# All scores of the first sequence in float32, from q and k laid out along partitions by the host

## The chip, the cores and the metric

The program runs on one core of a Trainium2 chip. A core has five engines that run their own instruction streams in order: TensorE (PE, matmuls; its weight loads are listed as PEld), VectorE (DVE), ScalarE (ACT), GpSimd (POOL) and SyncE (SP), which here issues nearly all DMAs. Engines wait for one another through semaphores. The metric is the device time of one execution in microseconds; the time of the kernel before is 735.77 us, the median of 3 runs (735.07 to 739.84).

## What is computed

Block-causal attention over 4 sequences with 8 heads, 576 rows and a head size of 64, then a dense layer of two matmuls with an ELU between them, then a top-1 mixture of 8 experts with a skip decision per row. Only the attention is touched here:

```python
B, H, S, D = q.shape                     # 4, 8, 576, 64
scores = scale * np.matmul(q, k.transpose(0, 1, 3, 2))     # scale 1/8
mask = block_i >= block_j                # blocks of 64 rows
scores = np.where(mask, scores, -1000000000.0)
scores = scores - np.max(scores, axis=-1, keepdims=True)
attn = np.exp(scores)
attn = attn / (np.sum(attn, axis=-1, keepdims=True) + 1e-09)
return np.matmul(attn, v).astype(np.float32)
```

Rows of the attention's result are put one sequence after the other into a matrix of 2304 x 512, which goes through the dense layer (512 to 2048 to 512) in 9 chunks of 256 rows.

## The kernel before

All instructions up to the experts are recorded first and then issued in an order that a planner chooses (`Recorder.order`): it knows what each step reads and writes, has an estimated duration for each kind of step, and gives each engine the step that can start first, with ties by the place in the program. Nearly every instruction thus carries the line of the recording helper, L320; rows are told apart by the names of tiles. A change of any step's cost, queue or buffer can move the order everywhere behind it.

**Attention.** A unit of `s_unit` (line 741) is one head of one 128-row tile n of queries (n = 0 to 3), or, for the last 64 rows (n = 4), a pair of heads, one in each half of the output's partitions. A pair p has two heads, and four pairs make the 8 heads. `x_unit` takes the maximum of a unit's scores (DVE, `mx`) and the exponential (ACT, `e`), `h_unit` and `l_unit` divide by the sum and split the result into two float16 halves (`ehl`, ACT and DVE), a transposing DMA turns them (`et`), and `pv` multiplies with the values (PE, `xps`), whose result is copied to `xt`, the input of the dense layer. Groups of units: g = 0 is n = 0 and 1 (rows 0 to 255, chunk 0 of the dense layer), g = 1 is n = 2 and 3 (chunk 1), and for sequence 0 g = 2 is n = 4.

**Scores by float16 halves.** For most tiles a row tile of q or k is loaded as it lies in memory (`raw`, 5 buffers), split into two float16 halves on ACT and DVE (`prep_k` writes `k1`, `prep_q` writes `qq`), and turned by a DMA transpose (`kt`, `qt`). The halves of 64 elements stand above each other in 128 partitions. For q a second copy with the halves swapped is made by two more DMAs (`qt<-qt`). Two matmuls per unit then give all four products of halves. The transposes and the swaps stand in SP's queue, in the planned order, with the loads of the dense layer's weights (`rw`), which come in an 8-byte format and are turned to float32 by three DVE instructions for each half (`twi`, `two`).

**Scores in float32.** For sequence 0 and n = 0 and 1 (`early`) the host hands over q and k of the first 256 rows once more, as `q0` and `k0` of 128 x 1024 with the two heads of a pair along the partitions. `load_early` (line 687) loads them without transposes. The q of one head is a tile whose other 64 partitions are zero, so that one float32 matmul with the k of both heads gives that head's scores. k of these rows is loaded and split to float16 as well (`prep_k`, b = 0, n = 0 and 1), since the tiles n = 2 to 4 need it.

**Dense layer.** For chunks 0 and 1 both matmuls run in float32 (`h<-xt,twi`, `y<-two,g`), from chunk 2 on in float16 halves of scaled weights. Chunk 1 can start when all four pairs of g = 1 have been multiplied with the values. Small matmuls `bm` and `cn` serve maxima and column norms for the scales, `lp` the routing. Sums of squares of weights (`sq`, `junk`) and of v (`vflat`) run on ACT.

## Time and profile before

| | |
|---|---|
| median of 3 runs | 735.77 us |
| the profiled execution | 739.56 us, its span 737.8 us |
| PE busy | 677.5 us (92%) |
| DVE busy | 575.0 us (78%) |
| ACT busy | 509.4 us (69%) |
| POOL busy | 79.3 us (11%) |
| moved by DMA | 133.99 MB |

Times in rows are microseconds from the span's start. PEclk is TensorE's granted clock as a share of full speed: 0.5 is the lower of two levels, and a value between is a mix over the stretch. A float32 matmul has two entries in the trace, so counts of float32 matmuls are twice those in the code. What stands in brackets behind a row is the time the engine stood idle before it and what ended that.

### The profile page before, as it was taken

Reading aid. Unit: us, or ns where it says so; the run is one execution under the profiler, and the core shown is the slowest. Engines: PE = TensorE matmul, PEld = TensorE weight load, DVE = VectorE, ACT = ScalarE, POOL = GpSimd, SP = SyncE. Lnnn points to the kernel's source line nnn. Section 1 sums busy time; section 2 is a strip of 40 time slices with the busy share of each in tenths; the row PEclk is TensorE's granted clock in tenths of the full one; section 3 lists DMA queues with packets and bytes.
Section 4 is the critical chain, followed back from the end, with each engine's and each line's share of the span. In section 5 each row is a group of like instructions: output and inputs, shape, how many; then the busy total and the mean of one; then the engine's idle time right before and its main releaser. Section 6 shows DMA issues by size and latency. Waiting matters only on the chain.

```text
span 737.8 us, 17507 instructions
## 1 busy us (share of the span) xinstructions
PE 677.5 (92%) x6553; PEld 466.8 (63%) x6553; DVE 575.0 (78%) x1646; ACT 509.4 (69%) x1086; POOL 79.3 (11%) x118
## 2 busy tenths in 40 slices
PE   6798984999989898989999999999999999999894
PEld 4585442776467656647657667667576677677683
DVE  5979898788989897888969965999778654675553
ACT  5755479899886886777758744767366556786682
POOL 1000000010000100100100010000106033323112
PEclk9799995799999999999999999999999999999998
DMA  9799999866798969979429447917065878998631
GB/s 299 247 259 282 387 270 234 179 142 138 155 176 144 185 154 211 169 142 202 91 42 176 98 59 206 376 58 226 32 201 145 222 162 195 218 275 150 224 117 16
DMA packets 213739, 133.99 MB, mean 182 GB/s; under 512 B 178171, under 2 KB 179205, under 8 KB 213120
## 3 DMA queue, kind: packets, MB, share of 16 engines
q1 hardware_dynamic: 208592, 123.85, 68.3%
q0 software_dynamic: 3952, 6.70, 4.5%
q10 hardware_dynamic: 1088, 2.10, 0.8%
q8 instruction: 56, 0.92, 0.5%
q14 instruction: 51, 0.42, 0.2%
HBM read 74.12 MB, written 12.75 MB: 118 GB/s over the span
## 4 chain that ended last, share of the span: by engine, by line
DMA 28%; PE 25%; issue 24%; DVE 14%; ACT 3%; SPq 2%; POOL 2%; POOLq 0%; DVEq 0%; ACTq 0%
PE h L320 10%; DMA out_dram<-o,gp 9%; PE y L320 8%; DMA gpa<-pay_d,ah 7%; DMA et<-ehl 4%; PE s L320 3%; DMA lst_d<-li,si 3%; PE xps L320 3%; DVE ehl L320 3%; DVE mx L320 2%; SPq L320 2%; DVE two L320 2%; DMA qt<-qt 2%; DVE twi L320 1%; DVE el L320 1%
## 5 line engine op out<-in xcount | busy, mean ns | idle before, releaser
L320 PE MATMUL h<-xt,win 128*128 128x256 f16 x1344 | 158.0, 273 | 1.0 <-DVE n L320 1.0
L320 PE MATMUL y<-wout,g 128*128 128x512 f16 x672 | 155.7, 379 | 0.0
L320 PEld LDWEIGHTS <-win 128*128 128x128 f16 x1344 | 129.0, 98 | 22.5 <-DVE n L320 1.1
L320 PEld LDWEIGHTS <-g 128*128 128x128 f16 x672 | 64.0, 98 | 66.6
L320 ACT ACTIVATE e<-s,mx 128x512 f32<-128x512 f32 (+4 forms) x160 | 82.0, 515 | 16.7 <-DVE ehl L320 6.9
L320 DVE TENSOR_REDUCE mx<-s 128x1 f32<-128x512 f32 (+4 forms) x160 | 74.7, 476 | 21.7 <-PE s L320 20.5
L320 ACT ACTIVATE ehl<-e,su 128x512 f16<-128x512 f32 (+4 forms) x144 | 74.0, 560 | 15.0 <-DVE su L320 9.0
L320 DVE SCALAR_TENSOR_TENSOR ehl<-e,su,ehl 128x512 f16<-128x512 f32 (+4 forms) x144 | 75.4, 552 | 3.3 <-ACT ehl L320 3.0
L320 PE MATMUL s<-kt,qt 128*128 128x384 f16 (+5 forms) x352 | 63.1, 314 | 11.8 <-ACT e L320 9.9
L320 PE MATMUL h<-xt,twi 128*128 128x256 f32 x256 | 64.6, 409 | 2.9 <-DVE g L320 2.7
L320 PE MATMUL y<-two,g 128*128 128x512 f32 x128 | 58.5, 599 | 0.6 <-DVE two L320 0.6
L320 PEld LDWEIGHTS h<-xt,twi 128*128 128x128 f32 x256 | 51.4, 206 | 11.8 <-DVE g L320 3.1
L320 ACT ACTIVATE el<-h,col 128x512 f32<-128x512 f32 x56 | 38.2, 683 | 25.5 <-PE h L320 24.1
L320 PEld LDWEIGHTS <-vt 128*64 128x64 f16 x1368 | 38.1, 115 | 24.2 <-issue 15.8
L320 PE MATMUL xps<-et,vt 128*64 128x128 f16 (+1 forms) x1368 | 46.6, 219 | 7.4 <-DMA et<-ehl 3.9
L320 PEld LDWEIGHTS <-p 128*128 128x128 f16 x984 | 46.6, 98 | 10.6 <-issue 4.7
L320 ACT ACTIVATE g<-el,col 128x512 f16<-128x512 f32 x56 | 40.2, 718 | 17.2 <-DVE el L320 16.7
L320 PEld LDWEIGHTS <-qt 128*128 128x128 f16 (+1 forms) x352 | 26.1, 105 | 32.2 <-issue 18.4
L320 DVE SCALAR_TENSOR_TENSOR g<-el,col,g 128x512 f16<-128x512 f32 x56 | 41.7, 745 | 2.5 <-ACT g L320 2.4
L320 DVE SCALAR_TENSOR_TENSOR el<-h,col,el 128x512 f32<-128x512 f32 x56 | 41.8, 746 | 1.2
L1531 DVE SCALAR_TENSOR_TENSOR p<-p,n,p 128x1024 f16<-128x1024 f32 x32 | 40.6, 1281 | 2.5 <-ACT p L1530 2.4
L320 DVE TENSOR_TENSOR hh<-r,hh 128x256 f16<-128x256 f32 x36 | 15.0, 424 | 33.5 <-ACT hh L1676 32.7
(236 smaller groups left out, 1152.6 us busy)
## 6 DMA issues: line engine op xcount, KB each, us to landing
p<-in_moe_w_dram SPq DMA_DIRECT2D x45, 512.0 KB
rw<-in_moe_w_in_dram SPq DMA_DIRECT2D x16, 512.0 KB
rw<-in_moe_w_out_dram SPq DMA_DIRECT2D x16, 512.0 KB
pb<-in_moe_w_dram SPq DMA_DIRECT2D x10, 512.0 KB
vflat<-in_v_dram SPq DMA_DIRECT2D x4, 1152.0 KB
out_dram<-pay SPq DMA_DIRECT2D x18, 256.0 KB
pay_d<-pay SPq DMA_DIRECT2D x18, 256.0 KB
raw<-in_k_dram SPq DMA_DIRECT2D x16, 256.0 KB
```

Of the source, the lines that this page charges most:

```text
L320: rec.call(e, time, lambda: getattr(self.real, op)(*args, **kw), reads, writes, dma)
L1531: rc.call("dve", 1.2, lambda: nc.vector.scalar_tensor_tensor(out=half(1), in0=raw.t, scalar=sc, in1=half(0), op0=ALU.mult, op1=ALU.subtrac ...
```

## The change

The short path of the first 256 rows is extended to all 576 rows of sequence 0. `q0` and `k0` are now 128 x 2304. `load_q0(n)` and `load_k0(n)` bring one row tile each; all of k is one float32 tile in the place that the float16 `kt` of sequence 0 had, and a q tile holds both heads, each with the other head's partitions zero (by DVE for n = 0 and 1, by POOL after that). `prep_k` for sequence 0 is only the scaling by 1/8 on ACT, `prep_q` nothing. In `s_unit` a unit of n < 4 is one float32 matmul and the one for the mask; a pair of n = 4 is one float32 matmul for each head and each of its two parts. The first v tile moves to the other ring of buffers (`ehl`).

```diff
--- before.py
+++ after.py
@@ -662,6 +662,9 @@
         return 128 if n < 4 else 64
 
     def load_raw(nm, b, n):
+        if b == 0 and nm != "v":
+            (load_q0 if nm == "q" else load_k0)(n)
+            return
         src = {"q": q, "k": k, "v": v}[nm]
         r = trows(n)
         t = ap.tile([128, H, D], F32, tag="raw", bufs=5, name="raw")
@@ -684,25 +687,36 @@
 
     X0 = {}
 
-    def load_early():
-
-        X0["q"] = [ap.tile([128, 2, 4, 128], F32, tag="qt", bufs=3, name="qx") for h in range(2)]
-        X0["k"] = ap.tile([128, 2, 4, 128], F32, tag="ehl", bufs=2, name="kx")
+    def load_q0(n):
+
+        r = trows(n)
+        x = QT[0, n] = ap.tile([128, 2, 4, r], F32, tag="qt" if n < 4 else "qh", bufs=3 if n < 4 else 1, name="qx")
         for h in range(2):
-            nc.vector.memset(X0["q"][h][64 - 64 * h:128 - 64 * h], 0.0)
+            (rc.gpsimd if n > 1 else nc.vector).memset(x[64 - 64 * h:128 - 64 * h, h], 0.0)
+        for h in range(2):
+            rows = slice(64 * h, 64 * h + 64)
+            rc.sync.dma_start(out=x[rows, h].rearrange("p a t -> p (a t)"), in_=q0[rows, 512 * n:512 * n + 4 * r])
+
+    def k0_of(n):
+        return KT[0][:, 512 * n:512 * n + 4 * trows(n)]
+
+    def load_k0(n):
+
+        if n == 0:
+            KT[0] = ap.tile([128, 4 * S], F32, tag="kt0", bufs=1, name="kx")
+        rc.sync.dma_start(out=k0_of(n), in_=k0[:, 512 * n:512 * n + 4 * trows(n)])
+
+    def load_v0():
+
+        x = X0["v"] = ap.tile([128, 2, H, D], F32, tag="ehl", bufs=2, name="vx")
         for n in range(2):
-            rows = slice(64 * n, 64 * n + 64)
-            rc.sync.dma_start(out=X0["q"][n][rows].rearrange("p n a t -> p (n a t)"), in_=q0[rows, :])
-            rc.sync.dma_start(out=X0["k"][:, n].rearrange("p a t -> p (a t)"), in_=k0[:, 512 * n:512 * n + 512])
-        X0["v"] = ap.tile([128, 2, H, D], F32, tag="qt", bufs=3, name="vx")
-        for n in range(2):
-            rc.sync.dma_start(out=X0["v"][:, n].rearrange("p h d -> p (h d)"), in_=v[0, 128 * n:128 * n + 128].rearrange("p h d -> p (h d)"))
-            RAW["v", 0, n] = X0["v"][:, n]
-
-    def scale_early(n):
-        rc.scalar.activation(out=X0["k"][:, n], in_=X0["k"][:, n], func=AF.Copy, scale=0.125)
+            rc.sync.dma_start(out=x[:, n].rearrange("p h d -> p (h d)"), in_=v[0, 128 * n:128 * n + 128].rearrange("p h d -> p (h d)"))
+            RAW["v", 0, n] = x[:, n]
 
     def prep_k(b, n):
+        if b == 0:
+            rc.scalar.activation(out=k0_of(n), in_=k0_of(n), func=AF.Copy, scale=0.125)
+            return
         r = trows(n)
         raw = RAW.pop(("k", b, n))
         if n == 0:
@@ -713,6 +727,8 @@
         rc.sync.dma_start_transpose(out=KT[b][:, :, n * 128:n * 128 + r], in_=k1[0:r].rearrange("p h a d -> p (h a d)"))
 
     def prep_q(b, n):
+        if b == 0:
+            return
         r = trows(n)
         raw = RAW.pop(("q", b, n))
 
@@ -744,16 +760,21 @@
         n = i // 2
         w = 128 * (n + 1) if n < 4 else S
         parts = [(0, w)] if w <= 512 else [(0, 512), (512, w)]
-        if not early(b, n):
-            qt, kt = QT[b, n], KT[b]
+        qt, kt = QT[b, n], KT[b]
         mx = sm.tile([128, 4], F32, tag="mx", bufs=4, name="mx")
         tl = []
         for m, (a, e_) in enumerate(parts):
             t = ps.tile([128, e_ - a], F32, tag="s", bufs=3, name="s")
             rc.atom()
-            if early(b, n):
-                rc.tensor.matmul(out=t, lhsT=X0["q"][i % 2][:, n, p, :], rhs=X0["k"][:, 0:n + 1, p, :], start=True, stop=False)
-                rc.tensor.matmul(out=t[:, w - 64:w], lhsT=later16[:, 0:128], rhs=later16[:, 128:192], start=False, stop=True)
+            if b == 0:
+                rhs = (kt[:, 0:512 * min(n + 1, 4)].rearrange("p (n a t) -> p n a t", a=4, t=128)[:, :, p, :] if m == 0
+                       else kt[:, 2048 + 64 * p:2112 + 64 * p])
+                if n < 4:
+                    rc.tensor.matmul(out=t, lhsT=qt[:, i % 2, p, :], rhs=rhs, start=True, stop=False)
+                    rc.tensor.matmul(out=t[:, w - 64:w], lhsT=later16[:, 0:128], rhs=later16[:, 128:192], start=False, stop=True)
+                else:
+                    for h in range(2):
+                        rc.tensor.matmul(out=t[64 * h:64 * h + 64, :], lhsT=qt[:, h, p, :], rhs=rhs, start=True, stop=True)
                 tl.append(t)
                 continue
             for ps_ in range(2):
@@ -1341,17 +1362,19 @@
 
     VF = [4, 5, 6, 6, 7, 8, 9]
     rc.base = -300
-    load_early()
+    load_q0(0)
+    load_k0(0)
+    load_q0(1)
+    load_k0(1)
+    load_v0()
     setup_consts()
     for x0, x1, y in ((0, 64, -2048.0), (64, 128, 0.0), (128, 192, 4096.0)):
         rc.gpsimd.memset(later16[:, x0:x1], y)
-    scale_early(0)
-    scale_early(1)
+    prep_k(0, 0)
+    prep_k(0, 1)
     rc.base = 0
     load_to(8)
     vflat(0)
-    addex(0, L("k", 0, 0), L("k", 0, 1))
-    addex(3, P(prep_k, 0, 0), P(prep_k, 0, 1))
     ex[6][0:0] = [lambda: vmax(0), lambda: vscale(0)]
     addex(9, P(prep_v, 0, 0), P(prep_v, 0, 1))
     for x in range(6):
@@ -1979,7 +2002,8 @@
     for name in _INS + ['q0', 'k0']:
         a = inputs[name[0] if name in ('q0', 'k0') else name]
         if name in ('q0', 'k0'):
-            a = a[0, :, 0:256].reshape(4, 2, 2, 128, 64).transpose(1, 4, 2, 0, 3).reshape(128, 1024)
+            a = a[0].reshape(4, 2, 9, 64, 64).transpose(1, 4, 0, 2, 3).reshape(128, 4, 576)
+            a = _np.concatenate([a[:, :, 128 * n:128 * n + 128].reshape(128, -1) for n in range(5)], 1)
         elif name in 'qkv':
             a = a.transpose(0, 2, 1, 3)
         a = _np.ascontiguousarray(a)
```

Three places of the order that the planner now makes, as the built programs have it (buffer numbers are kept in some names). First SP's queue behind the first weights: `rw` are weights, `raw` tiles of q, k or v as they lie in memory, `kx` and `qx` those in float32. Before:

```order
L320 DMA vflat<-in_v_dram 128x2304
L320 DMA raw<-in_k_dram 128x512 x3
L320 DMA raw<-in_q_dram 128x512
L320 DMA rw<-in_moe_w_in_dram 128x2x512
L320 DMA raw<-in_v_dram 128x512
L320 DMA rw<-in_moe_w_in_dram 128x2x512
L320 DMA_TRANSPOSE kt<-k_172 128x8x128
L320 DMA_TRANSPOSE qt<-qq 128x8x128
L320 DMA raw<-in_k_dram 64x512
L320 DMA rw<-in_moe_w_in_dram 128x2x512 x2
L320 DMA raw<-in_k_dram 128x512
L320 DMA_TRANSPOSE kt<-k_173 128x8x128
```

The same queue, after:

```order
L320 DMA vflat<-in_v_dram 128x2304
L320 DMA kx<-in_k_dram 128x512
L320 DMA qx<-in_q_dram 64x512 x2
L320 DMA rw<-in_moe_w_in_dram 128x2x512
L320 DMA raw<-in_v_dram 128x512
L320 DMA kx<-in_k_dram 128x256
L320 DMA rw<-in_moe_w_in_dram 128x2x512
L320 DMA qx<-in_q_dram 64x256 x2
L320 DMA raw<-in_v_dram 64x512
L320 DMA rw<-in_moe_w_in_dram 128x2x512 x2
L320 DMA kx<-in_k_dram 128x512
L320 DMA raw<-in_v_dram 128x512
```

All q and k of sequence 0 are in the queue with the first weights, and the transposes of k and q that stood between weight loads are gone. Second, PE around the start of chunk 0 (`h<-xt,twi`), before:

```order
L320 MATMUL tp<-ident,en 128x128 x4
L320 MATMUL xps<-et,vx 64x128 x4
L320 MATMUL h<-xt,twi_174 128x256 x8
L320 MATMUL h<-xt,twi_207 128x256 x8
L320 MATMUL h<-xt,twi_238 128x256 x8
```

and after:

```order
L320 MATMUL tp<-ident,en 128x128 x4
L320 LDWEIGHTS ones_75
L320 MATMUL bm_189<-bmt,ones_75 128x1
L320 MATMUL xps<-et,vx 64x128 x4
L320 MATMUL s<-kx,qx 128x384
L320 LDWEIGHTS late
L320 MATMUL s<-late 128x64
L320 MATMUL h<-xt,twi_170 128x256 x8
L320 MATMUL h<-xt,twi_198 128x256 x4
L320 MATMUL s<-kx,qx 128x512
L320 LDWEIGHTS late
L320 MATMUL s<-late 128x64
```

A score unit of n = 2 (384 columns; two more stand a little ahead of these rows) is now in front of chunk 0, and units of n = 3 (512 columns) follow in the second of its eight steps, where before the first unit of n = 2 stood in the sixth and the first of n = 3 behind three of eight steps of y. Third, PE between the last y of chunk 0 and the 42 value products ahead of chunk 1. Before, the products follow these rows:

```order
L320 MATMUL lp<-wgs,x2t 128x9
L320 LDWEIGHTS ones_75
L320 MATMUL cn<-cb,ones_75 128x8
L320 LDWEIGHTS qt
L320 MATMUL s<-kt,qt 128x128
L320 LDWEIGHTS late
L320 MATMUL s<-late 128x64
L320 LDWEIGHTS qt
L320 MATMUL s<-kt,qt 128x128
```

and after, these:

```order
L320 MATMUL y<-two_362,g 128x512 x2
L320 MATMUL bm_322<-ident,col 1x128
L320 MATMUL s<-kx,qx 64x512 x2
L320 MATMUL bm_325<-ident,col 1x128
L320 MATMUL s<-kx,qx 64x64 x2
L320 LDWEIGHTS ones_75
L320 MATMUL bm_324<-bmt,ones_75 128x1
L320 LDWEIGHTS ones_75
L320 MATMUL cn<-cb,ones_75 128x8
L320 MATMUL s<-kx,qx 64x512 x2
L320 LDWEIGHTS ones_75
L320 MATMUL bm_327<-bmt,ones_75 128x1
```

Before, routing (`lp`) and the first scores of sequence 1 came ahead of these products, and all four pairs of n = 4; now the last y of chunk 0 is twelve rows ahead of them, with three and a half of the four pairs of n = 4 in front.

## Rows read from the trace of the kernel before

**Rows 1.** By stretches: stretch, length, busy time and count by engine, granted clock, DMA

```profile
core 0: us, PE busy (x) PEld busy (x) DVE busy (x) ACT busy (x) POOL busy (x), PEclk, DMA share, GB/s
0.00:32.00 32.00, 20.84 (x122) 13.43 (x122) 23.82 (x78) 20.72 (x62) 3.95 (x38) 0.91 0.84 292
32.00:60.00 28.00, 27.81 (x123) 23.20 (x121) 23.42 (x45) 14.46 (x28) 0.00 (x0) 0.93 0.92 241
60.00:80.00 20.00, 16.79 (x61) 9.30 (x60) 17.65 (x35) 8.28 (x16) 0.00 (x0) 0.91 1.02 310
80.00:106.00 26.00, 23.96 (x117) 11.20 (x119) 24.88 (x54) 19.00 (x36) 0.00 (x0) 1.00 1.09 335
106.00:134.70 28.70, 15.79 (x217) 10.56 (x217) 22.36 (x98) 25.50 (x62) 0.61 (x3) 0.59 1.09 233
134.70:140.00 5.30, 5.30 (x20) 4.32 (x16) 3.99 (x17) 4.26 (x10) 0.20 (x1) 0.63 1.04 212
140.00:200.00 60.00, 60.00 (x448) 39.57 (x447) 52.51 (x141) 55.95 (x130) 3.42 (x4) 1.00 0.68 143
```

**Rows 2.** PE's timeline: start, duration, what, count [idle time before, its end]

```profile
32.02 21.29 PE L320 MATMUL h<-xt,twi 128*128 128x256 f32 x88
...
62.75 5.41 PE L320 MATMUL h<-xt,twi 128*128 128x256 f32 x16 [2.74 <-DVE g L320]
...
80.67 0.59 PE L320 MATMUL s<-kt,qt 128*128 128x512 f16 x2 [1.15 <-DMA qt<-qt]
...
102.28 3.70 PE L320 MATMUL y<-two,g 128*128 128x512 f32 x8 [0.20 <-DVE two L320]
...
129.55 2.45 PE L320 MATMUL xps<-et,vt 128*64 128x128 f16 x42
...
134.69 5.62 PE L320 MATMUL h<-xt,twi 128*128 128x256 f32 x16
```

**Rows 3.** PE's timeline: score units in float32 and in float16

```profile
15.88 0.49 PE L320 MATMUL s<-kx,qx 128*128 128x128 f32 x2
...
16.23 0.69 PE L320 MATMUL s<-kx,qx 128*128 128x256 f32 x2
...
21.01 0.69 PE L320 MATMUL s<-kx,qx 128*128 128x256 f32 x2
...
21.57 0.68 PE L320 MATMUL s<-kx,qx 128*128 128x256 f32 x2
...
53.15 0.33 PE L320 MATMUL s<-kt,qt 128*128 128x384 f16 x1
...
53.86 2.75 PE L320 MATMUL h<-xt,twi 128*128 128x256 f32 x12
```

**Rows 4.** PE's timeline: float32 value products in half arrays; scores of n = 4

```profile
13.87 0.44 PE L320 MATMUL xps<-et,vx 128*64 128x128 f32 x4
...
16.88 0.66 PE L320 MATMUL xps<-et,vx 128*64 128x128 f32 x8
...
110.54 0.62 PE L320 MATMUL s<-kt,qt 128*64 128x512 f16 x4
...
111.20 0.30 PE L320 MATMUL s<-kt,qt 128*64 128x64 f16 x4
```

**Rows 5.** Groups of instructions from 0 to 140: busy time, mean ns of one

```profile
L320 ACT ACTIVATE sq<-twi 128x1024 bf16<-128x1024 f32 x8 | 8.4, 1045 | 0.1
...
L320 DVE SCALAR_TENSOR_TENSOR k<-raw,k 128x512 f16<-128x512 f32 x7 | 4.8, 684 | 0.0
...
L320 ACT ACTIVATE k<-raw 128x512 f16<-128x512 f32 x7 | 4.3, 620 | 0.2 <-DMA kt<-k 0.2
```

**Rows 6.** Chain of waits in order of time: start, duration, what

```profile
70.61 9.93 DMA qt<-qt
...
121.98 4.42 DMA et<-ehl
```

**Rows 7.** SP's timeline: issue of the first k tile

```profile
1.46 0.57 SPq L320 DMA_DIRECT2D kx<-in_k_dram  x1
```

## The prediction

> **What bounds the kernel now.** I read the kernel by stretches first, then the order of matmuls on TensorE (PE) inside them, then the chain of waits. From 140 us on PE is the bound: in the next 60 us it is busy all the time at full clock [rows 1], so what happens ahead of that is worth what it delays PE. Ahead of it PE loses time in two ways that add up: it stands idle, and its clock falls. I count both as lost time: a stretch minus its busy time times its granted clock. From [rows 1] this gives 13.0 us for 0 to 32 (32 - 20.84 x 0.91), 2.1 for 32 to 60, 4.7 for 60 to 80, 2.0 for 80 to 106, 19.4 for 106 to 134.7 and 2.0 for 134.7 to 140: 43.2 us in all. The rows of PE show what the stretches are [rows 2]. At 32.02 chunk 0 of the first expert layer starts (h, then y) and ends at 106; chunk 1 starts at 134.69, right behind the 42 value products (xps) of the last head pair of rows 256 to 511. So the 19.4 us are a wait of chunk 1 for attention. Inside chunk 0 two stalls stand out: 2.74 us on a VectorE (DVE) result and 1.15 us on the swapped q of row tile 3 [rows 2].
>
> Why is attention late? The chain of waits has a piece of 9.93 us that ends when the swap DMAs of that q land, and later a transposing DMA of 4.42 us [rows 6]. The scores of tile 3 could thus start only at 80, and everything behind them (maximum, exponential, split, transpose, value product) was pressed into 80 to 131. Meanwhile DVE was busy 88.3 of the 102.7 us of 32 to 134.7 (the sum of four stretches of [rows 1]), ScalarE (ACT) 25.5 of the last 28.7, and the DMA queues had a share of 0.84 to 1.09 from the start.
>
> **What the change costs PE.** Float32 scores take one product instead of two, but it is slower by column. A float32 unit of 128 columns takes 0.35 us (15.88 to 16.23), one of 256 0.56 (21.01 to 21.57): 0.21 per 128 columns [rows 3]. So 384 columns cost 0.77 and 512 cost 0.98. Two float16 units of 384 columns fill 53.15 to 53.86, 0.355 each [rows 3]; scaled by columns one of 512 is 0.47. With eight units of each width: 8 x (0.77 - 0.355) + 8 x (0.98 - 0.47) = 7.4 us more. Row tile 4 has four units of 576 columns in which two heads use half of the array each. The float32 value products have that form: four entries take 0.44 us, eight 0.66 [rows 4], so one 128-column product on both halves costs 0.22, and a unit 4.5 x 0.22 + 0.2 = 1.2. If the halves did not overlap it were 2.0. The float16 unit took 0.62 + 0.30 = 0.92 in a stretch with a granted clock of 0.59 [rows 1, 4]; at the higher of the two levels I estimate 0.65. That is 4 x 0.55 = 2.2 more, between 1.1 and 5.4. Sum: **9.6 us** (8.5 to 13) of added PE work.
>
> **What it removes elsewhere.** For sequence 0 five k tiles and three q tiles need no split: eight DVE instructions of 0.684 us (5.5 us) and eight on ACT of 0.620 (5.0 us, less three scalings of k that are new, 1.6 by their columns) [rows 5]. Eight transposing DMAs and six swaps leave SP's queue; of the loads, the pieces of q and k come as float32 in their final layout. SP ran in order, and the order of before shows weight loads (rw) and raw tiles standing behind the first k and q transposes; these are now plain loads with nothing ahead of them that waits for a computed half. Here the Trainium skill (Advanced Engine Details and Errata, section X-Bar Transpose) says that transposing DMAs are as fast as plain ones, 350 to 400 GB/s. By that rule the eight transposes are 1.8 MB and 5 us of queue time. The trace isolates no transpose in an empty queue: its 4.42 us for 393 KB [rows 6] is longer than the 1.1 that the rule gives, in a queue with other loads in it.
>
> **What moves, stretch by stretch.**
> *0 to 32.* q now comes in two loads per tile where there was one, so the first k is issued third instead of second, and the second k sixth instead of fourth. One issue takes about 0.6 us [rows 7] and PE's first scores wait for these tiles, so I add 1 us (0 to 1.2). On ACT, ahead of the last copy of chunk 0's input, the new order puts three sums of squares of 1.05 us [rows 5], two scalings of k (1.0 together, by the row of the k split and their columns) and two exponentials (1.2, likewise), and takes away two splits (1.2): 4.1 us net. ACT is busy 20.72 of 32 us [rows 1], so part of it falls into its gaps. With the first 1 us I estimate that h starts 3 us later. Three float32 scores of 0.77 fill 2.3 of these, which leaves 0.7. The stretch loses 13.0 + 1.7 = 14.7 (13 to 18).
> *Chunk 0.* The waits on q and, with DVE relieved just where its k and q splits stood around 61 us, most of the 2.74 us go: 8.8 becomes 5; I add 1 for score units that now sit between h and y and wait for their score buffers. 6 (3 to 10).
> *The gap before chunk 1.* Scores of tile 3 start beside h, not at 80, so three of the four pairs are through their value products before y ends. What is left is the last pair: its split, a transpose of about 4.4 us, 42 products. In the new order these 42 stand behind four small matmuls of the maxima (bm, cn), which wait for DVE and ACT results of the pay tile and of tile 4: about eight ACT instructions, an estimated 6 us by the widths and [rows 5], in parallel with the transpose. I take 5 us for gap and clock together, against 21.4 before; bounds 3 (the chain is early) and 21 (nothing is gained).
> *After it.* Routing, the first scores of sequence 1 and the vector work of two units of tile 4 are now behind the start of chunk 1: by the order an estimated 2 us of PE, 7 of DVE and 5 of ACT work. In 140 to 200 DVE is busy 52.5 of 60 us and ACT 55.95 [rows 1], so DVE's share just fits and ACT's not quite: 1.5 us (0 to 4).
>
> **The sum.** Lost time 14.7 + 6 + 5 + 1.5 = 27.2 against 43.2: 16.0 us won. Minus 9.6 of added PE work: 6.4 us less. The profiled execution took 739.56 us (span 737.8 and 1.8 around it), 3.8 above the median of 735.77. The same difference on the median gives 735.77 - 6.4 = **729 us**. About 1% (7.4 us) is what a measurement of this kernel can tell from no change, so the forecast lies at the edge of that.
>
> **The rivals.**
> *More is gained.* If nothing stalls chunk 0 and the last pair is early, the lost time is 14 + 4 + 3 = 21, the gain 22.2 - 9.6 = 12.6, the time 723. For it: DVE's queue loses 5.5 us where it was busy nine tenths. Against it: ACT's new early work.
> *The gap is ACT's, not q's.* In 106 to 134.7 ACT was busy 25.5 of 28.7 us, and the change takes only 3.4 us from it in all. If ACT's queue paces the last pair, the gap shrinks only to about 11.5; 33.7 lost, 9.5 won, 9.6 paid: 736, no change. Against it: from 32 to 80 ACT was busy only 22.7 of 48 us [rows 1], and scores that come earlier let its work move there. The rule of the Trainium skill on transposes speaks for this rival too, since by it the removed DMAs were cheap.
> *Slower.* The added PE work stands in front of the chain it should help: the last pair's scores lie on PE behind y and behind 5 to 6 us of longer scores, and its chain of maximum, exponential, split and transpose begins only then. If the gap stays as it was (the total lost time is 43 again), the 9.6 us are paid in full: 745. The point that decides is where chunk 1's first h stands. Before, it is at 134.69 with 2.0 us of slow clock behind it; afterwards the 2 us of moved PE work and the 1.5 above still follow. So it is break-even at about 133; the forecast puts it at 127; at 140.6 or later the kernel is slower by 1%.
>
> **How the numbers follow.** Forecast (725 to 734) 0.45; more gained 0.22; no change 0.20; slower 0.13. Faster by over 1% (below 728.4) takes all of the second and a good third of the first: 0.39. Slower by over 1% (above 743.1) takes most of the last: 0.11. Within 1%: 0.50. The range 721 to 741 leaves out the far end of the second and most of the last, under 0.2.
>
> **What would show it.** Right: chunk 0's h starts at about 35 behind three float32 scores; units of 384 and 512 columns at 0.77 and 0.98; no wait for a q DMA in chunk 0; y ends at 114 to 120; h of chunk 1 at 124 to 130 with a granted clock near 1 around it. Wrong: h starting after 38 (ACT's early work), a y stage with PE waiting for DVE or for score buffers, the 42 products held by the small matmuls beyond 132, units of tile 4 of 2 us, or idle time of PE between 130 and 200, where it had none from 134.7 on.

## The result, and the profile after

The changed kernel takes **714.99 us** (median, 714.26 to 716.24) where the kernel before took 735.42 (734.25 to 739.84): a ratio of 0.971 with a 95% interval of 0.968 to 0.975, 20.4 us less. Timed again beside the later experiments it was 0.975 (0.970 to 0.980). The forecast was 729 with a range of 721 to 741: the sign was right, the size was off by a factor of three. The profiled execution took 23.3 us less (a span of 714.5 for 737.8); that of before was one of its slower ones, which is where the 3 us between 23.3 and 20.4 lie.

The first rows are those of the changed kernel by stretches, cut where chunk 0 begins (38.1), where its last y ends (112.5), where chunk 1's first h stands (118.4), where the float16 chunks begin (194.4) and where their last h ends (547.6). They answer to [rows 1].

```profile
core 0: us, PE busy (x) PEld busy (x) DVE busy (x) ACT busy (x) POOL busy (x), PEclk, DMA share, GB/s
0.00:38.10 38.10, 26.44 (x132) 16.64 (x132) 27.19 (x86) 25.24 (x73) 6.59 (x44) 0.87 0.95 303
38.10:112.50 74.40, 74.40 (x376) 45.77 (x374) 68.01 (x148) 48.80 (x96) 0.00 (x0) 1.00 0.98 273
112.50:118.40 5.90, 4.46 (x62) 2.27 (x61) 5.00 (x31) 3.69 (x9) 0.41 (x2) 1.00 1.03 239
118.40:194.40 76.00, 75.25 (x587) 48.24 (x587) 69.24 (x212) 71.86 (x174) 5.25 (x6) 1.00 0.76 157
194.40:547.60 353.20, 347.10 (x3403) 236.86 (x3402) 304.37 (x921) 246.43 (x535) 26.31 (x36) 1.00 0.67 159
547.60:714.50 166.90, 151.02 (x2004) 115.02 (x2002) 94.78 (x247) 108.45 (x197) 43.37 (x37) 0.96 0.70 176
```

The same cut of the kernel before, for the part behind 134.7 that the prediction did not look at closely:

```profile
134.70:209.50 74.80, 73.99 (x522) 47.76 (x519) 65.62 (x176) 68.16 (x158) 3.83 (x6) 0.97 0.71 149
209.50:569.40 359.90, 347.15 (x3403) 237.38 (x3402) 302.32 (x919) 244.75 (x531) 26.69 (x35) 1.00 0.67 155
569.40:737.80 168.40, 151.16 (x2004) 113.99 (x2002) 94.91 (x247) 108.47 (x197) 44.21 (x37) 0.97 0.71 175
```

In the changed kernel TensorE (PE) is busy without a gap and at full clock through all of chunk 0, and the wait before chunk 1, 28.7 us long before, is 5.9 us with 4.5 of them work. Something else stands lower down: the float16 chunks have the same PE work in both (347.1 us), but waits of 12.75 us before (359.9 - 347.15) and 6.1 after.

Lost time (a stretch minus busy time times granted clock, as in the prediction) sums up as follows. The clock changes inside some stretches, so here each is taken in pieces of 2 us, which moves single values by up to 3 us against the rows.

| lost time, us | before | forecast | after | after, again |
|---|---|---|---|---|
| up to h of chunk 0 | 13.2 | 14.7 | 16.1 | 16.2 |
| chunk 0 | 9.1 | 6 | 0.0 | 0.0 |
| wait before chunk 1 (before: with the 1.9 of slow clock behind it) | 21.1 | 5 | 1.4 | 0.5 |
| rest of chunk 1 | 0.8 | } 1.5 more | 0.8 | 0.9 |
| float16 chunks | 12.8 | } than before, | 6.1 | 7.6 |
| end | 18.8 | } together | 18.9 | 18.5 |
| sum | 75.8 | | 43.3 | 43.7 |
| PE's work (busy time times clock) | 662.0 | +9.6 | 671.2 | 673.1 |

32.5 us of lost time less, 9.2 us of work more: 23.3 us.

PE's timeline answers to [rows 2 to 4] (start, duration, what, count, idle time before it and its end):

```profile
38.10 5.43 PE L320 MATMUL h<-xt,twi 128*128 128x256 f32 x24
43.36 1.02 PE L320 MATMUL s<-kx,qx 128*128 128x512 f32 x2
...
44.25 1.10 PE L320 MATMUL s<-kx,qx 128*128 128x512 f32 x2
...
47.03 0.81 PE L320 MATMUL s<-kx,qx 128*128 128x384 f32 x2
...
47.70 20.97 PE L320 MATMUL h<-xt,twi 128*128 128x256 f32 x96
...
112.68 1.08 PE L320 MATMUL s<-kx,qx 128*64 128x512 f32 x4
...
113.89 0.34 PE L320 MATMUL s<-kx,qx 128*64 128x64 f32 x4
...
115.67 0.16 PE L320 MATMUL bm<-bmt,ones 1*128 1x1 bf16 x1 [1.44 <-ACT pay L320]
...
116.99 1.36 PE L320 MATMUL xps<-et,vt 128*64 128x128 f16 x42
118.28 0.27 PE L320 MATMUL bm<-ident,col 128*1 128x128 f32 x1
118.39 1.97 PE L320 MATMUL h<-xt,twi 128*128 128x256 f32 x8
```

A unit of 512 columns takes 0.89 us (43.36 to 44.25), one of 384 takes 0.67 (47.03 to 47.70), one of tile 4 about 1.3 (1.01 to the next matmul for its 512 columns, 0.27 to 0.34 for its 64). Chunk 0 starts 6 us later than before, chunk 1 starts 16.3 us earlier.

Work that stood ahead of the old wait has moved forward. VectorE (DVE) rounds the float32 weights of the second layer (`two`) from what SP has loaded (`rw`); its last such rows, of before and of after:

```profile
100.35 2.48 DVE L320 SCALAR_TENSOR_TENSOR two<-rw,two 128x512 int32<-128x512 int32 x4
```

```profile
93.43 0.69 DVE L320 SCALAR_TENSOR_TENSOR two<-rw,two 128x512 int32<-128x512 int32 x1
```

Before, it stood right among the work of the last head pairs and ended at 102.8, 3 us before y; after, it ends at 94.1, 18 us before y. The loads of weights leave SP earlier too; whether that is the cause is taken up below. The last loads of first-layer weights (SP's timeline, before and after):

```profile
50.58 1.09 SPq L320 DMA_DIRECT2D rw<-in_moe_w_in_dram  x2
```

```profile
32.98 3.06 SPq L320 DMA_DIRECT2D rw<-in_moe_w_in_dram  x4
```

What did PE stand for in the old wait? Of the 19.2 us lost from 106 to 134.7 it was idle for 12.9, and the rest is slow clock. 6.2 us of the idle time, in four pieces, came ahead of scores of tile 4 and ended with an exponential of ACT's that had read the scores before them (all scores share three buffers). 2.8 us came ahead of the routing (`lp`) and ended when a transposing DMA of its input had landed. The largest pieces, in PE's timeline of the kernel before:

```profile
116.37 1.17 PE L320 MATMUL s<-kt,qt 128*64 128x512 f16 x8 [2.72 <-ACT e L320]
...
124.98 0.32 PE L320 MATMUL s<-kt,qt 128*64 128x64 f16 x4 [2.39 <-ACT e L320]
127.61 0.48 PE L320 MATMUL lp<-wgs,x2t 128*128 128x9 f16 x12 [2.31 <-DMA x2t<-pay]
```

Before chunk 1 of the changed kernel PE is idle only for the 1.44 us shown above. ACT has done more when y ends: it is busy for 48.8 us of chunk 0, where it was for 41.7 (the sum of three rows of [rows 1]).

### The profile page after: what moved, and what is told of

Read it like the earlier page. It is cut to its first block, busy times and chain, and to the rows that moved or that the text cites. A ratio compares the mean times of both kernels' runs of the same rounds, so it can differ in the third digit from the quotient of the medians.

```text
span 714.5 us, 17462 instructions
## 1 busy us (share of the span) xinstructions
PE 678.7 (95%) x6553; PEld 464.8 (65%) x6553; DVE 568.6 (80%) x1640; ACT 504.5 (71%) x1081; POOL 81.9 (11%) x124
## 3 DMA queue, kind: packets, MB, share of 16 engines
HBM read 73.59 MB, written 12.75 MB: 121 GB/s over the span
## 5 line engine op out<-in xcount | busy, mean ns | idle before, releaser
L320 DVE TENSOR_REDUCE mx<-s 128x1 f32<-128x512 f32 (+4 forms) x160 | 75.3, 477 | 16.6 <-PE s L320 16.0
L320 ACT ACTIVATE ehl<-e,su 128x512 f16<-128x512 f32 (+4 forms) x144 | 74.1, 561 | 12.9 <-DMA et<-ehl 4.0
L320 DVE SCALAR_TENSOR_TENSOR ehl<-e,su,ehl 128x512 f16<-128x512 f32 (+4 forms) x144 | 75.8, 552 | 6.0 <-ACT ehl L320 5.8
L320 PE MATMUL h<-xt,twi 128*128 128x256 f32 x256 | 59.2, 384 | 0.3 <-DVE g L320 0.3
L320 PEld LDWEIGHTS h<-xt,twi 128*128 128x128 f32 x256 | 47.3, 190 | 7.9 <-issue 1.0
L320 PEld LDWEIGHTS <-vt 128*64 128x64 f16 x1368 | 35.4, 111 | 22.8 <-issue 15.7
L320 PE MATMUL s<-kt,qt 128*64 128x512 f16 (+5 forms) x288 | 48.7, 298 | 0.7 <-ACT e L320 0.5
L320 PE MATMUL xps<-et,vt 128*64 128x128 f16 (+1 forms) x1368 | 44.1, 213 | 3.9 <-DMA et<-ehl 2.2
L320 DVE SCALAR_TENSOR_TENSOR g<-el,col,g 128x512 f16<-128x512 f32 x56 | 41.7, 745 | 3.3 <-ACT g L320 3.0
L320 PE MATMUL s<-kx,qx 128*128 128x128 f32 (+5 forms) x96 | 34.7, 523 | 7.6 <-ACT kx L320 6.7
L320 POOL DMA_INDIRECT lst_d<-li,si x16 | 19.3, 1209 | 188.5 <-DVE li L320 90.6
```

The source lines that it names most:

```text
L320: rec.call(e, time, lambda: getattr(self.real, op)(*args, **kw), reads, writes, dma)
```

## The experiments

Ratios are to the kernel before on the same chip. "Wait" is the lost time between y's end and chunk 1's h, in pieces of 2 us as above.

### Is it that q comes too late?

In two runs q of row tile 3 is held back in the changed kernel, by zero fills on GpSimd (105 and 52) ahead of the load. In the third the planner knows their duration, and tile 2 is late as well.

```
+ if n == 3 and h == 0:
+     for _ in range(105):
+         rc.gpsimd.memset(x[64:128, 0], 0.0)
```

The second run has 52 in place of 105. The third has 52 for tile 2 and 50 for tile 3, in this form:

```
+         rc.call("pool", 0.40, ..., [QT[0, 2][64:128, 0]] if n == 3 else [], [x[64:128, 0]])
```

> The changed kernel, with the q of row tile 3 of sequence 0 held back: 105 more zero fills of 0.5 us on GpSimd, idle there, stand ahead of the fill that its load waits for, so that it lands at about 80 us, where the swapped q of the kernel before landed, instead of about 36. Splits and transposes stay away. Theory 'late q' (the wait of chunk 1 came from the late operands of tile 3): chunk 1's h goes from 118.4 back to 127 to 135 and the kernel to 724 to 734. Theory 'relief' (what helped is that VectorE, ScalarE and SP do less): the scores of tile 3 still fit, chunk 1's h stays at 118 to 122, 714 to 719.

> The same with half of the delay (52 fills): q of tile 3 lands at about 53 us. Theory 'late q', if what matters is how much of chunk 0 is left beside the scores: little, 715 to 719, since y begins only at 68. If each microsecond of delay counts: half of the price of the longer delay. Theory 'relief': 714 to 716.

> The changed kernel with q of row tile 2 landing at about 53 us and q of tile 3 at about 80, as in the kernel before, again by zero fills on GpSimd ahead of the loads; this time the planner is given their duration, so that it writes other work in front of the scores that come late, where the two earlier delays made TensorE stand in front of them. No splits, transposes or swaps come back. Theory 'early operands' (VectorE and ScalarE have attention work from 36 us on and are through when y ends): the wait before chunk 1 comes back, chunk 1's h at 128 to 136, 724 to 734. Theory 'amount of work' (10.5 us of splits fewer is what empties these queues): h at 118 to 122, 714 to 719.

Measured: 1.025 (1.020 to 1.030), 0.994 (0.991 to 0.997) and 0.994 (0.990 to 0.997); so 14 to 17 us more than the changed kernel for the short delay and 36 to 39 for the long one. The first lies beyond everything expected. The second costs 0.4 of the first, near the half that was expected if each microsecond counts. The third lies in the range of 'early operands', but its mark, the late chunk 1 behind a wait, is missing. In all three the place was another: the wait before chunk 1 stayed at 0.8, 0.6 and 1.5 us. PE stood at the first late score, inside chunk 0 or, in the planned run, partly ahead of it. PE's timeline of the long delay, of the short one, and of the planned one:

```profile
86.45 2.07 PE L320 MATMUL s<-kx,qx 128*128 128x512 f32 x2 [31.06 <-POOL qx L320]
```

```profile
55.00 2.08 PE L320 MATMUL s<-kx,qx 128*128 128x512 f32 x2 [13.34 <-POOL qx L320]
```

```profile
38.59 1.65 PE L320 MATMUL s<-kx,qx 128*128 128x384 f32 x2 [4.19 <-POOL qx L320]
...
70.02 2.08 PE L320 MATMUL s<-kx,qx 128*128 128x512 f32 x2 [3.55 <-POOL qx L320]
```

PE runs in the order that was written, so an operand that comes later than the order assumes is paid 1:1 and more (18 us between the two rows, 23 between the two kernels). It does not by itself bring back the wait before chunk 1. The planned version still stood in these places, so it is no clean copy of a late q that the order allows for.

### Tile 3 first, with halves

In the kernel before, the preparation of tile 3 is written ahead of that of tile 4 for sequence 0.

```
+ a_, c_ = (3, 4) if b == 0 else (4, 3)
- addex(g0 + 4, P(prep_k, b, 2), P(prep_q, b, 2), L("v", b, 2), L("k", b, 4))
+ addex(g0 + 4, P(prep_k, b, 2), P(prep_q, b, 2), L("v", b, 2), L("k", b, a_))
...
- addex(g0 + 14, P(prep_q, b, 3))
+ addex(g0 + 14, P(prep_q, b, c_))
```

> The kernel before, with halves, transposes and swaps, in which only the preparation of row tile 3 of sequence 0 (loads, splits, transposes, swaps) is written ahead of that of tile 4 instead of behind it. Theory 'late q': tile 3's q lands 10 to 20 us sooner, the wait of chunk 1 shrinks by 8 us or more and the kernel takes 715 to 728 with the old, shorter scores. Theory 'relief' (or that the float32 operands themselves matter): no gain over 4 us, 732 to 738.

Measured: 0.989 (0.984 to 0.994), 727.5 us. The kernel gains 8 us, and yet not as expected:

```profile
106.60:134.70 28.10, 13.77 (x207) 9.44 (x205) 19.76 (x94) 22.92 (x56) 0.61 (x3) 0.59 1.11 229
...
208.30:560.50 352.20, 346.12 (x3404) 237.35 (x3402) 303.67 (x920) 246.29 (x535) 27.22 (x35) 1.00 0.69 158
```

The wait before chunk 1 is as long as it was [rows 1]: 28.1 us with a clock of 0.59. And yet q of tile 3 did come early. Its first scores stand at 61.1, 18 us sooner than before (79.1), and the swapped q is there at 62.4, where it was at 80.7 [rows 2]:

```profile
62.43 0.59 PE L320 MATMUL s<-kt,qt 128*128 128x512 f16 x2 [0.95 <-DMA qt<-qt]
```

The scores of tile 4 begin no later for it (109.6, 110.5 before). So with halves an early q of tile 3 does not shorten the wait, and in the changed kernel a late one does not bring it back. The gain of this run stands mostly in the float16 chunks, which lose 6.1 us (352.2 - 346.12), as in the changed kernel, and here with halves.

### Putting the removed work back, dead

The splits of sequence 0 (eight on DVE, eight on ACT) come back with nobody using them; then the eight transposing DMAs and six swaps with them; then the DMAs without the splits (sources filled on GpSimd); then plain copies of the same bytes for the transposes. For room, the ring of raw tiles has four buffers instead of five wherever DMAs come back, so a run has only that.

```
+ k1 = ap.tile([128, H, 2, D], F16, tag="k1", bufs=1, name="k1")
+ rc.scalar.activation(out=k1[0:r, :, 0, :], in_=src, func=AF.Copy, scale=0.25)
+ rc.vector.scalar_tensor_tensor(out=k1[0:r, :, 1, :], in0=src, scalar=0.25, in1=k1[0:r, :, 0, :], op0=ALU.mult, op1=ALU.subtract)
+ rc.sync.dma_start_transpose(out=dead_t()[:, :, 0:r], in_=k1[0:r].rearrange("p h a d -> p (h a d)"))
...
- t = ap.tile([128, H, D], F32, tag="raw", bufs=5, name="raw")
+ t = ap.tile([128, H, D], F32, tag="raw", bufs=4, name="raw")
```

> The changed kernel with the eight splits of k and q of sequence 0 put back on VectorE and ScalarE as dead work (their float16 halves are used by nothing; no transpose, no swap): 5.5 us more on VectorE, 5.0 on ScalarE, where the kernel before had them. Theory 'relief': at least 6 us of the 20 come back, 720 to 727. Theory 'late q': 714 to 718.

> The changed kernel with the whole preparation of q and k of sequence 0 put back as dead work: the eight splits, the eight transposing DMAs and the six swap DMAs, whose results nothing uses (for their room the ring of raw tiles has four buffers in place of five). With the dead splits alone the kernel took 719.3 us. Theory 'queue' (SP's issues, 1.3 us for a transpose, and the DMA queue's load count): 3 us or more on top, 722 to 730. If what counted was only that scores wait for these DMAs: 718 to 721, the same as with the dead splits.

> The changed kernel with four raw tiles in the ring in place of five and nothing else: the part of the dead preparation that was only there for room. If the dead preparation's price was its own: 0.967 to 0.975 of the kernel before, as the changed kernel (0.971). If the ring was part of it: 0.976 to 0.982.

> The changed kernel with the eight transposing DMAs and six swaps put back as dead work, without the splits: their sources are filled on GpSimd, which is idle there (ring of four raw tiles). With splits and DMAs the ratio to the kernel before was 0.986, with the splits alone 0.977, with neither 0.971. Theory 'the DMAs cost by themselves': 0.978 to 0.984. Theory 'they cost only together with the splits (SP stands at a transpose until its split is done)': 0.970 to 0.975.

> The same as the run with the dead DMAs, but each of the eight transposing DMAs is a plain copy of the same bytes from tile to tile. If a transpose is as cheap for the queue as a plain copy (the rule of the Trainium skill, Advanced Engine Details and Errata, section X-Bar Transpose): the same time as with the transposes, within 2 us. If transposes are what is dear: at least 3 us less than with them, near the changed kernel (0.971 to 0.975).

| | ratio (interval) | h of chunk 1 | wait |
|---|---|---|---|
| changed kernel | 0.971 (0.968 to 0.975), 0.975 (0.970 to 0.980) | 118.4, 117.6 | 1.4, 0.5 |
| ring of four alone | 0.981 (0.978 to 0.985) | 122.6 | 2.6 |
| splits | 0.977 (0.973 to 0.982) | 119.7 | 5.7 |
| DMAs | 0.987 (0.984 to 0.991) | 127.8 | 10.6 |
| splits and DMAs | 0.986 (0.981 to 0.991) | 129.9 | 11.4 |
| plain copies | 0.991 (0.988 to 0.994) | 128.3 | 12.5 |

The stretch before chunk 1 in the run with splits, and in the one with DMAs:

```profile
108.60:119.70 11.10, 8.84 (x103) 5.10 (x102) 10.30 (x55) 9.85 (x26) 0.41 (x2) 0.65 0.82 199
```

```profile
110.90:127.80 16.90, 10.46 (x109) 5.59 (x107) 12.01 (x58) 14.24 (x34) 0.41 (x2) 0.70 1.06 230
```

Three things follow. DMAs whose results nobody uses bring back about half of the old wait (10.6 us, against 2.6 with their ring alone), and add 4.4 us to the run with their ring (0.006; the intervals overlap a little, but each of its four runs is slower than each of the ring's four; the ring of four is not free either); the splits alone bring 4 us of wait and at most a few us of time, and on top of the DMAs nothing that these intervals show. The prices don't add up. And transposes aren't dear among DMAs: with plain copies of the same bytes the kernel is no faster. The Trainium skill says just that (Advanced Engine Details and Errata, section X-Bar Transpose: transposing DMAs run as fast as plain ones); by the time of the kernel these runs agree with it. The queue's rows show what a transpose does differ in (with transposes, then with copies: packets, MB, share of the span):

```profile
q1 hardware_dynamic: 208640, 123.33, 69.6%
```

```profile
q1 hardware_dynamic: 202240, 123.33, 67.9%
```

6,400 packets more for eight transposes, and 504 us of queue time (69.6% of 724.4) against 496 (67.9% of 730.2), about 1 us each.

A part of this price may be the experiment's own. All dead results share one buffer (tag `dead`), so SP, which issues in order, stands until the dead DMA before has landed. From 10 to 105 us SP stood for 18.4 us for dead DMAs in the run with DMAs, and for 7.0 more for the fills on GpSimd. The two largest entries (what SP waited for, us in total, times, longest):

```profile
SPq L320 <- DMA dead<-qx: 8.9, 3, 4.3
SPq L320 <- DMA dead<-k: 8.1, 4, 3.3
```

In the same stretch of the kernel before, SP stood for the split of q:

```profile
SPq L320 <- DVE qq L320: 12.7, 2, 10.0
```

The plain copies tell against the buffer as the whole price: there SP waited only 3.7 us for dead DMAs and 3.3 for fills, and the wait before chunk 1 is 12.5 us.

### What do the DMAs hold back?

With the dead DMAs the last first-layer weights leave SP at 46.78 instead of 32.98 (32.76 with their ring alone):

```profile
46.78 1.10 SPq L320 DMA_DIRECT2D rw<-in_moe_w_in_dram  x2
```

But late weights are not all of it. With plain copies the last first-layer weights also leave late, at 44.42, and still the rounding of the second layer ends at 95.5, 1.4 us later than in the changed kernel; the wait is the longest of the table. DVE's last such row there:

```profile
94.83 0.69 DVE L320 SCALAR_TENSOR_TENSOR two<-rw,two 128x512 int32<-128x512 int32 x1
```

Then the weight loads were taken off SP: the last 24 of 32 leave from GpSimd's queue, in the kernel before, in the changed one, and in the one with dead DMAs. In a fourth run the dead copies and swaps leave from GpSimd and the weights stay on SP.

```
- rc.sync.dma_start(out=dst, in_=src)
+ if x < 8:
+     rc.sync.dma_start(out=dst, in_=src)
+ else:
+     rc.call("pool", 1.0, lambda: nc.gpsimd.dma_start(out=dst, in_=src), [src], [dst], 4.0)
```

> The kernel before (halves, splits, transposes, swaps), in which the last 24 of the 32 weight loads leave from GpSimd's queue, idle there, instead of SP's. Theory 'weights behind SP': their rounding ends about 93 instead of 103, chunk 1's h comes at 120 to 128 instead of 134.7, and the ratio is 0.975 to 0.99. Theory 'it only goes with it' (what counts is late q and k, and the work of splits): 0.995 to 1.01.

> The changed kernel with the same 24 weight loads on GpSimd's queue. Since its wait before chunk 1 is 1.4 us already, little is left to win: 0.965 to 0.975, as the changed kernel, or up to 3 us less where SP's issues of transposes come sooner. If loads from this queue are dearer (VectorE and GpSimd share a port, or the start is delayed): 0.975 to 0.985.

> The kernel with the eight dead transposes and six dead swaps, and the weight loads on GpSimd's queue. Theory 'weights behind SP': most of the DMAs' price goes, chunk 1's h from 127.8 to 119 to 122, 0.970 to 0.978. Theory 'the DMAs load the queue itself or hold back the transposes of e': 0.983 to 0.99, as with the loads on SP (0.987).

> The kernel with the eight dead copies and six dead swaps, all issued by GpSimd instead of SP (ring of four raw tiles); issued by SP it took 0.991 of the kernel before, and without them, with that ring, 0.981. Theory 'SP's order': SP is as free as in the changed kernel, so 0.978 to 0.985, with the wait before chunk 1 at 4 us or less. Theory 'load on the DMA engines': they still move these bytes, 0.987 to 0.995, with the wait at 8 us or more.

Measured: 1.002 (0.998 to 1.006), 1.003 (0.999 to 1.006), 1.026 (1.018 to 1.033), 0.999 (0.996 to 1.003). Only the first lies in a range that was expected ('it only goes with it'), and it doesn't test that theory, since the weights were rounded no earlier. In the kernel before, with its weights on GpSimd's queue, their last rounding on DVE ends at 113.95; it had ended at 102.8, and 93 was expected:

```profile
111.46 2.49 DVE L320 SCALAR_TENSOR_TENSOR two<-rw,two 128x512 int32<-128x512 int32 x4
```

In the changed kernel it ends at 104.8 (94.1 before the move), with dead DMAs at 119.1. In the first two q came late as well, and in the third PE stood mostly for ACT (9.3 and 7.1 us). PE's timeline of the kernel before and of the changed kernel, each with its weights on GpSimd's queue:

```profile
88.48 1.01 PE L320 MATMUL s<-kt,qt 128*128 128x512 f16 x2 [4.68 <-DMA qt<-qt]
```

```profile
45.60 2.04 PE L320 MATMUL s<-kx,qx 128*128 128x512 f32 x2 [9.30 <-DMA qx<-in_q_dram]
```

The DMA share is 0.84 to 0.92 up to 60 us in the kernel before [rows 1] and 0.95 up to 38 us in the changed one, and both the weights and q came later. The fourth run fell to a buffer: ACT's squares of the weights share one tile (tag `k1`) with the dead k and stood for the slow copy (ACT's timeline), and PE behind them for 13 us. Its wait before chunk 1 is 1.0 us, but behind those 13, so it decides between neither theory.

```profile
79.49 1.06 ACT L320 ACTIVATE sq<-twi 128x1024 bf16<-128x1024 f32 x1 [18.05 <-DMA dead<-k]
```

So it stays open whether SP's order, the load on the DMA engines or the one buffer carries the price of the fourteen DMAs. That the dead work carries one is shown, the way it takes is not: late first-layer weights go along with it, but the plain copies speak against the rounding of the second layer as the link, and no run separates the rest.

### What TensorE's added work costs

```
+ if n in (2, 3):
+     rc.tensor.matmul(out=t, lhsT=qt[:, i % 2, p, :], rhs=rhs, start=True, stop=True)
```

> The changed kernel with every float32 score product of row tiles 2 and 3 computed twice into the same place: 16 products more, 0.72 us each for 384 columns and 0.93 for 512, so 13 us of TensorE work. If TensorE is the bound of chunk 0 throughout: 727 to 729, all of it paid. If part of it falls into waits that the trace shows as busy time, or buys VectorE and ScalarE time: 718 to 725.

Measured: 0.994 (0.991 to 0.998), 14 to 17 us more than the changed kernel, and 734.4 us. PE's work grew by 12.9 us to 684.1, as expected; chunk 1's h came 10.4 us later (128.8), since 2.5 us of slow clock fell away ahead of chunk 0. Chunk 0 had nothing to hide it in:

```profile
38.30:121.30 83.00, 83.00 (x403) 50.33 (x403) 69.36 (x148) 50.77 (x100) 0.41 (x2) 1.00 0.94 257
```

The rest lies in the float16 chunks, which lost 11.6 us where the changed kernel lost 6.1 and 7.6, and in the last stretch, which lost 27.7 us in this profile where others lose 15 to 22.

### The order of the rest

Four runs say what an order is worth behind chunk 1: the changed kernel again; the kernel before with one number of the planner altered (first piece); and two tries at chunk 0's late start, with the squares of the weights made to depend on chunk 0's first product (second piece), and with k scaled on GpSimd (third).

```
-    slack = 0.2
+    slack = 0.4
...
+        for s in rc.steps[x:]:
+            if s[0] == "act":
+                s[4].add(H0[0])
...
+            if n > 1:
+                rc.gpsimd.tensor_scalar(out=k0_of(n), in0=k0_of(n), scalar1=0.125, scalar2=None, op0=ALU.mult)
```

> The changed kernel, nothing altered, on the chip of these three: 0.968 to 0.975 if its ratio holds from chip to chip, and the float16 chunks lose about 6 us again if that is the order's and not the run's.

> The kernel before with one number of the planner changed, the slack by which an urgent step may be late (0.4 for 0.2), which alters the order only from the last chunks of the first expert layers on. It prices the luck of an order: the second expert layers' first part (the float16 chunks) lost 12.8 us before and 6.1 after, where the change has no work of its own. If that difference is the order's luck: this kernel moves by 2 to 8 us either way (0.99 to 1.01), with its waits elsewhere. If an order is worth under 1.5 us: 0.998 to 1.002.

> The changed kernel in which the sums of squares of the first-layer weights on ScalarE (eight, 1.05 us each, three of which stood ahead of chunk 0's input) may only begin behind the first product of chunk 0. If these three delayed chunk 0's start: h at 33 to 36 instead of 38.1 and 710 to 713. If the start is set by something else, or the squares now come late for the second layer of the gap: 714 to 717.

> The changed kernel with the three new scalings of k (row tiles 2 to 4) on GpSimd instead of ScalarE, which loses 1.6 us of work ahead of chunk 0. If ScalarE's queue sets chunk 0's start: h at 35 to 37 instead of 38.1, 0.966 to 0.973. If GpSimd's scaling (and its use of VectorE's port) comes later than ScalarE's did, or the planner only fills the gap with other work: 0.973 to 0.98.

Measured: 0.975 (0.970 to 0.980), 1.007 (1.004 to 1.010), 0.980 (0.975 to 0.985), 0.977 (0.970 to 0.984). The float16 chunks in these four runs, in that order:

```profile
193.60:548.40 354.80, 347.22 (x3403) 237.00 (x3402) 304.53 (x921) 246.74 (x535) 27.04 (x36) 1.00 0.67 159
```

```profile
212.30:572.70 360.40, 347.27 (x3404) 237.27 (x3403) 302.79 (x920) 245.60 (x532) 24.43 (x33) 1.00 0.67 154
```

```profile
195.00:555.30 360.30, 349.20 (x3406) 238.23 (x3405) 304.68 (x921) 247.44 (x537) 27.08 (x36) 1.00 0.67 156
```

```profile
193.80:554.10 360.30, 350.16 (x3405) 238.95 (x3403) 304.23 (x923) 247.83 (x535) 27.86 (x36) 0.99 0.69 159
```

The altered number moved PE's order only from its 4,409th of 6,553 matmuls in the trace on (at 550 us in the kernel before), so up to there that run repeats the kernel before: 13.1 us of waits in the float16 chunks (360.4 - 347.27) and 19.7 ahead of chunk 1, as before. The changed kernel repeats its 6.1 with 7.6. The same order thus gives nearly the same waits. Another order with the same float32 scores gives 12.8 (squares) and 13.0 (k scaled), in pieces of 2 us; another one with halves gave 6.1. So these 6 to 7 us don't belong to the float32 scores. They are the luck of the order that the planner wrote with them. Over the twenty profiles of this case the float16 chunks lose between 5.5 us (the ring of four) and 13.1.

The squares did what was expected of them at their place (chunk 0 at 34.8 instead of 38.1), and the time came back as 4.5 us of wait before chunk 1 and in the float16 chunks. Scaling k on GpSimd left chunk 0 at 38.8. Neither is a faster kernel; none of the runs beats the changed one.

## Why the prediction was wrong

**Added work: right.** 9.6 us forecast, 9.2 measured (11.1 in the second profile of the changed kernel). A unit of 384 columns takes 0.67 to 0.78 us (0.77 forecast), one of 512 takes 0.89 to 0.97 (0.98), and one of tile 4 takes about 1.3 (1.2), so the two halves of the array overlap.

**0 to 32: a little too good.** Chunk 0 starts at 38.1, not 35, and above 38 the prediction had called itself wrong here; 16.1 us are lost instead of 14.7. Three float32 scores and three squares stand ahead of it, as said.

**Chunk 0: mis-sized by 6 us.** 6 forecast, nothing measured. The term that failed is the 1 us "for score units that wait for their score buffers" and the 5 us of waits left over from q, DVE and the old order. All of them went.

**The gap: mis-sized by 3.6, and misread.** 5 forecast, 1.4 measured, and h of chunk 1 at 118.4, not 127. The step that failed is the one from tile 3's q, landing at 80, to the wait of chunk 1. With halves and the first scores of tile 3 18 us sooner the wait lost 19.8 us, against 19.2 before, and with q held back in the changed kernel it stayed below 2. Inside the old wait PE stood mostly for ACT's exponentials and for the routing, and not for q. So that this term came out within 4 us is in part luck. What was left out is a price for the fourteen DMAs that leave the queues: put back dead, they alone lengthen the wait by 8 us over their ring's (y ends 4.5 us sooner there) and delay chunk 1 by 5 us, with the reservation about their buffer above. The prediction names the weight loads that stand behind the transposes, and gives them no term. (Its transpose of 4.42 us stands behind the split of tile 3, which is 524 KB by its two heads of 512 columns in two halves, not 393; the sum doesn't use the size.) Its rival "the gap is ACT's, not q's" (736) had the right engine in the old wait. It was rightly held less likely, since ACT's work did move into chunk 0 (48.8 us there against 41.7); but one of its grounds, that the removed DMAs were cheap, was wrong in this kernel.

**After it: the largest miss, 8 us.** 1.5 us more were forecast, because moved work would crowd ACT; with the slow clock of chunk 1 set aside, the later stretches lost 6.5 less, all of it in the float16 chunks (12.8 to 6.1), and the runs show that they come and go with the planner's order, with halves and without. The forecast treated everything behind 200 us as fixed. It was not, and nothing in the profile of before could have given the sign; but waits of 12.75 us in a bound stretch could have been read from it, and belonged in the range.

Together: 6.0 + 3.6 + 8.0 + 0.4 (work) - 1.4 (start) = 16.6 us, which with the forecast 6.4 make 23.0 of the 23.3. "More is gained" (723) had the mechanism of the first two and the right sign for chunk 0, and still stopped 8 us short.

What stays open: how the DMAs' price arises, and what made the rest of the old wait (21 us, against 11.4 with all dead work put back). One rival was not tested: the place of the routing in PE's order. It stands ahead of chunk 1's h in the kernel before and in the three runs with dead DMAs on SP, behind it in the changed kernel, with the splits and with the ring alone; with plain copies PE stood 4.25 us for it.

## What to carry to other kernels

A list of waits prices only what waits. DMAs whose results nobody used moved the next chunk by 5 us here, so give work that leaves a busy queue a term of its own. A late operand early in a chain is not yet the cause of a wait at its end: look at what the engine stands for inside that wait, and make the operand early alone. Where a planner writes the order, price the waits far behind the change too, and keep their whole size (here 6 to 13 us) in the range. Operands that come later than the order assumes are paid nearly 1:1, and moving loads to another queue made both them and others late here, with DMA shares of 0.84 to 0.95.

## What the runs showed of the hardware

The clock. In the changed kernel the granted clock stood at 0.50 to 0.51 (the lower level, 1.2 GHz) from 28 to 32 us, right behind 2 us in which PE was busy for 0.92; a unit of 384 columns took 1.60 us there (30.44 to 32.04) instead of 0.67. In the run with dead splits PE was busy only 0.94 and 0.63 of 2 us in 24 to 28, and kept the full clock. The rows of the changed kernel, then of that run:

```profile
26.00:28.00 2.00, 0.92 (x8) 0.51 (x8) 2.00 (x6) 2.00 (x6) 0.00 (x0) 1.00 1.07 367
28.00:30.00 2.00, 1.73 (x10) 1.01 (x10) 1.69 (x3) 1.81 (x7) 0.00 (x0) 0.51 1.05 283
30.00:32.00 2.00, 1.57 (x4) 0.65 (x3) 1.82 (x6) 2.00 (x2) 0.00 (x0) 0.50 1.07 245
```

```profile
24.00:26.00 2.00, 0.94 (x12) 0.61 (x10) 2.00 (x7) 2.00 (x6) 0.00 (x0) 1.00 1.05 269
26.00:28.00 2.00, 0.63 (x5) 0.20 (x6) 2.00 (x5) 2.00 (x4) 0.00 (x0) 1.00 1.06 362
28.00:30.00 2.00, 1.75 (x13) 1.02 (x13) 2.00 (x7) 2.00 (x5) 0.36 (x1) 1.00 0.98 247
```

Plain copy and transpose. A plain copy of 256 KB from tile to tile costs the kernel no less than the transposing DMA of the same bytes (ratios of 0.991 and 0.987 with eight of them).
